# Window attention and two MLPs on one core: the last two weight pairs take turns over the token groups, and the first activations of the last product are loaded and made behind the last units

## The chip, the cores and the metric

The program runs on one core of a Trainium2 chip, in one launch. The metric is device microseconds (us) of that core, from the start of an execution to its end. The kernel before takes 907.42 us, the median of three runs (906.17 to 907.88).

## The reference, cut

```python
# q, k, v: 4 x 8 heads x 576 x 64; scale 1/8
mask = (rel >= 0) & (rel < 64)                  # rel = query position - key position
attn = softmax(where(mask, scale * q @ k.T, -1e9))
x = (attn @ v) -> 2304 tokens x 512
h = x @ w_in;  x = maximum(0.01 * h, h) @ w_out         # MLP 1: 512 -> 2048 -> 512
h = x @ w_in2; g = maximum(h, 0) + log1p(exp(-abs(h)))  # MLP 2: softplus
out = g @ w_out2                                        # 2048 -> 512
```

All inputs are float64 on the host. The kernel reads the weights as 64-bit words and makes two parts out of each number, a high one (type fp32r) and a low one, so that a product of two numbers takes three matmuls on TensorE: high by high, high by low, low by high (`three`, L469 to L471).

## The kernel before, in words

**Stages.** First the attention and MLP 1, mixed with each other; then the first product of MLP 2 (x by w_in2); then its second product (softplus of that, by w_out2). The change touches the end of the first product and the start of the second.

**The first product, by units.** The 2048 columns of h stand in 16 blocks of 128, two of which are a *pair* (p = 0 to 7). The 2304 tokens stand in three groups of 768 (c = 0 to 2). A *unit* is one pair on one group: `products(n, p, c)`, L526, 24 units in the order of a list written by hand (from L711 on): six units of pairs 0 and 1 mixed, then pair by pair with the three groups of each. A unit multiplies a 2 by 2 block matrix with seven half-size products instead of eight (L535 to L556); each product is 6 matmuls of 384 columns into a PSUM bank of its own, so a unit is 42 matmuls on TensorE, and takes it 7.33 us. The banks are eight, in turns (L531). What leaves the banks: one copy by ScalarE (`q1`, L547) and seven additions by VectorE (L545; `u2`, `u3`, `v` and four that write the unit's result h). The result goes to DRAM (`hd[p]`, L557, issued on SyncE's queue). The inputs of group c stand in seven wide tiles, `XB[c]` (`xb_c_n`), the seven weight combinations of a pair in `wp_..` rows (`pair_rows`, L208; made by `conv_pair`).

**The blocks of w_out2.** Behind and among the last units, the 16 row blocks of w_out2 (128 x 512 each) are converted, block j in four steps by a `ticker` (`last`): `load_w` (a DMA on SyncE's queue, L133, into one of three buffers `raw64`), `conv_a` (ScalarE, L159; reads the raw words, writes `cvp`), `conv_b` (VectorE: a shift L170 and an addition of the low word L176), `conv_c` (`split`: ScalarE casts the high part, L222, VectorE subtracts it from the number, L223). `conv_a` has two forms. As long as no softplus has been placed in the program (`softplus_on` is empty) it is an activation by a table, L159, that keeps the sign. Later it is a multiplication, L161, and `conv_b` then has one more VectorE instruction, L172, that puts the sign in. The places of the two parts come from `w2_rows`, L189: blocks 0 to 2 in two tiles of their own, blocks 3 to 5 in small buffers left over from the attention and the pairs (`pair_rows(8)`), the others in wide tiles `w2_n`, three rows in each. There are 21 wide places in all (`WIDE`), and a new wide tile takes the place of an older one, once the readers of that one are done.

**The second product, by steps.** The tokens stand in four chunks of 512 and one of 256; a step is one chunk and one block j, 80 steps (`second`, L584). A step of 512 tokens is 12 matmuls of 512 columns (L469 to L471, tile `f`). Its input is made by `load_h` (L568: 128 x 512 of `hd`, DRAM to `s0`, on SyncE's queue) and `activate` (L573): VectorE sets the sign bit (L576), ScalarE does the softplus of minus the absolute value (L577), VectorE adds max(h, 0) (L579), and then comes a `split` (L222 on ScalarE, L223 on VectorE). The tiles for it (`s0` to `s5`, six wide places) are taken in `second_places`, L559. Activations run SKEW = 2 steps ahead of `second`, loads three more.

**What sets the order.** Each engine runs its own queue, in order. A scheduler puts the instructions into the queues as the program issues them, by when it takes their inputs to be ready. `later` (L669) issues a piece of work no earlier than the end of the evacuation of the unit LAG2 = 3 behind. In the kernel before, `second_places`, all loads of `s0` and all activations are issued after the loop over the units.

In profile rows, a name with numbers left out stands for all tiles of the name: `cvp` a block in conversion, `w2xh` and `w2_n` its parts, `p_a`, `p_s` the banks of a unit, `q`, `u`, `h_xl` what comes out of them, `s` the tiles of the activations, `f` the banks of the second product.

Of the kernel before, what the change touches and what calls it, by code (L numbers as in the profile page):

```python
# [20 lines left out]
def tile_window_attention_two_mlps(  # L21
# [31 lines left out]
    NT, DM = out.shape  # L53
# [3 lines left out]
    NF = DFF // P  # L57
# [5 lines left out]
    SKEW = 2  # L63
# [6 lines left out]
    NX = NT // (2 * TH)  # L70
    TO = 512
# [116 lines left out]

    def w2_rows(j):  # L189


        if j < 3:
            if j == 0:
                w_rows["x"] = [x_tile(nm, f"w2{nm}", [P, 3, DM], F32R) for nm in ("xh", "xl")]
            return [w[:, j] for w in w_rows["x"]]
        if j < 6:
            if j == 3:
                w_rows["a"] = pair_rows(NF // 2)
            return [w.rearrange("p a b -> p (a b)") for w in w_rows["a"][2 * (j - 3) : 2 * (j - 3) + 2]]
        rows = []  # L200
        for n in (2 * (j - 6), 2 * (j - 6) + 1):
            if n % 3 == 0:
                w_rows["w", n // 3] = wide(f"w2_{n // 3}")
            rows.append(w_rows["w", n // 3][:, n % 3])
        return rows

    def pair_rows(p):

        row = lambda tag, bufs, n: sb.tile(
            [P, n, 2, DM // 2], F32R, tag=tag, bufs=bufs, name=f"wp_{p}_{tag}{len(got)}"  # L210
        )
        got = []
        tags = (("v", 3, 1), ("kT", 2, 1), ("qbd", 1, 2), ("part", 1, 3))
        if p % 2 == 0:
            tags = (("raw", 2, 1),) * 2 + (("v", 3, 1),) * 2 + (("sm", 2, 1),) * 2 + (("kT", 2, 1),)
        for tag, bufs, n in tags:
            t = row(tag, bufs, n)
            got += [t[:, i] for i in range(n)]
        return got
# [339 lines left out]
    def second_places():  # L559
        h, g, gh, gl, r0, r1 = (  # L560
            wide(f"s{n}", F32R if n in (2, 3) else F32) for n in range(6)
        )
        rows = lambda t: [t[:, n] for n in range(3)]
        stage["in"], stage["g"] = turns(rows(h)), turns(rows(g))
        stage["gs"] = turns(list(zip(rows(gh), rows(gl))))
        stage["res"] = turns(rows(r0) + rows(r1))

    def load_h(t0, n, j):  # L568
        h = next(stage["in"])[:, :n]
        nc.sync.dma_start(h, hd[j // 2][:, j % 2, t0 : t0 + n])  # L570
        return h
# [137 lines left out]


    order = [(0, 0), (0, 1), (1, 0), (0, 2), (1, 1), (1, 2)]  # L711
    order += [(p, c) for p in range(2, NF // 2) for c in range(NX)]
    last_of = {p: max(n for n, (q, _) in enumerate(order) if q == p) for p in range(NF // 2)}
    todo = {n: [] for n in range(len(order))}
    todo[0] += [(load_x, 2, 0)]
# [2 lines left out]
    for p in range(2, NF // 2):  # L718
# [1 line left out]
        todo[n - 1] += [(next, first[p])] * 4  # L720
        todo[n] += [(next, first[p], None)] * 2
        todo[n + 1] += [(conv_pair, p)]
    for n, k in ((-6, 4), (-5, 2), (-3, 4), (-2, 4), (-1, 4)):
        todo[len(order) + n] += [(next, last)] * k
    for n, (p, c) in enumerate(order):
        products(n, p, c)
        for f, *a in todo[n]:
            later(f, *a)

    chunks = [(t0, min(TO, NT - t0)) for t0 in range(0, NT, TO)]  # L730
    steps2 = [(k, t0, n, j) for k, (t0, n) in enumerate(chunks) for j in range(NF)]
    loaded, active = {}, {}
    second_places()
    for i in range(-3, len(steps2) + SKEW):
        if 0 <= i < len(steps2):
            active[i] = activate(steps2[i][2], loaded.pop(i))
        if i + 3 < len(steps2):
            k, t0, n, j = steps2[i + 3]
            loaded[i + 3] = load_h(t0, n, j)
        if i >= 0:  # L740
            for _ in range(2):
                later(next, last, None)
        if i >= SKEW:
            second(*steps2[i - SKEW], active.pop(i - SKEW))


# [28 lines left out]
```

## Time and profile before

| | |
|---|---|
| median of three runs | 907.42 us (906.17 to 907.88) |
| the profiled execution's own time | 906.67 us |
| its span, first to last instruction | 904.6 us |
| TensorE matmuls (PE) busy | 870.0 us, 96% |
| TensorE weight loads (PEld) busy | 818.4 us, 90% |
| VectorE (DVE) busy | 538.2 us, 59% |
| ScalarE (ACT) busy | 419.7 us, 46% |
| GpSimd (POOL) busy | 47.7 us, 5% |
| mean granted TensorE clock | 0.985 |

The profile is of one execution, and its span is 2.07 us shorter than that execution's time. The busy shares are means over stages that differ. The views read below are the page's clock line, the list of who an engine waits for, the timelines of single engines, and a table of busy times by stretches of the span.

### The profile page before, as it was taken

How to read it: one execution, taken by the hardware profiler on the slowest of the kernel's cores; microseconds unless marked ns; L12 is line 12 of the kernel's file. 1: busy time of each engine (PE TensorE's matmuls, PEld its weight loads, DVE VectorE, ACT ScalarE, POOL GpSimd, SP SyncE). 2: the span in 40 equal slices, each digit the busy share in tenths (PEclk: the TensorE clock that was granted, in tenths of full speed). 3: DMA queues.
4: the chain of work that ended last, by engine and by line, in shares of the span. 5: the costliest groups of instructions: out<-in, count | busy, mean ns of one | idle time of the engine just before them, and what ended most of it. 6: DMA issues, size and time to landing. Idle time of an engine off the chain costs nothing.

```text
span 904.6 us, 14252 instructions
## 1 busy us (share of the span) xinstructions
PE 870.0 (96%) x5232; PEld 818.4 (90%) x5232; DVE 538.2 (59%) x1055; ACT 419.7 (46%) x990; POOL 47.7 (5%) x66
## 2 busy tenths in 40 slices
PE   5699999999999999999999999999995999999998
PEld 4498999999999999999999999999995788888886
DVE  3898852534333333333257599777889767667664
ACT  4888752654444443543446433222235544544443
POOL 2211000211100101100000000000000000000000
PEclk8899999999999999999999999999998899999999
DMA  6667742243232311110132245444667434344432
GB/s 174 182 183 219 233 107 33 73 72 76 48 56 53 84 48 46 48 24 1 37 129 80 95 153 186 151 151 152 216 226 279 129 94 141 102 141 117 126 99 67
DMA packets 150277, 104.74 MB, mean 116 GB/s; under 512 B 104896, under 2 KB 129472, under 8 KB 150208
## 3 DMA queue, kind: packets, MB, share of 16 engines
q1 hardware_dynamic: 150208, 103.84, 39.9%
q8 instruction: 41, 0.67, 0.3%
q14 instruction: 28, 0.23, 0.1%
HBM read 75.50 MB, written 28.31 MB: 115 GB/s over the span
## 4 chain that ended last, share of the span: by engine, by line
PE 93%; DVE 2%; DMA 2%; ACT 2%; issue 1%; POOL 0%; POOLq 0%; DVEq 0%; ACTq 0%; SPq 0%
PE ph L469 7%; PE f L469 7%; PE f L471 7%; PE f L470 7%; PE o L469 7%; PE o L470 7%; PE o L471 7%; PE ph L470 7%; PE ph L471 7%; PE ps L382 4%; PE p_s L469 4%; PE p_s L471 4%; PE p_s L470 4%; PE p_a L469 3%; PE p_a L471 3%; PE p_a L470 3%
## 5 line engine op out<-in xcount | busy, mean ns | idle before, releaser
L485 DVE TENSOR_TENSOR gl<-g,gh 128x384 fp32r<-128x384 f32 x96 | 58.6, 611 | 159.1 <-ACT gh L484 158.6
L469 PE MATMUL ph<-xh,w 128*128 128x384 f32 x384 | 132.3, 345 | 0.0
L469 PE MATMUL o<-gh,w 128*128 128x384 f32 x384 | 131.7, 343 | 0.0
L470 PE MATMUL o<-gl,w 128*128 128x384 f32 x384 | 129.8, 338 | 0.0
L470 PE MATMUL ph<-xl,w 128*128 128x384 f32 x384 | 129.0, 336 | 0.0
L471 PE MATMUL ph<-xh,w 128*128 128x384 f32 x384 | 128.8, 335 | 0.0
L471 PE MATMUL o<-gh,w 128*128 128x384 f32 x360 | 121.7, 338 | 0.0
L481 ACT ACTIVATE g<-ph 128x384 f32<-128x384 f32 x96 | 46.9, 489 | 134.6 <-PE ph L471 134.5
L577 ACT ACTIVATE s<-s 128x512 f32<-128x512 f32 (+1 forms) x80 | 46.8, 588 | 75.2 <-DVE s L576 74.6
L579 DVE SCALAR_TENSOR_TENSOR s<-s,s 128x512 f32<-128x512 f32 (+1 forms) x80 | 50.7, 638 | 42.5 <-ACT s L577 42.3
L469 PEld LDWEIGHTS ph<-xh,w 128*128 128x128 f32 x384 | 72.1, 188 | 0.9
L470 PEld LDWEIGHTS ph<-xl,w 128*128 128x128 f32 x384 | 72.2, 188 | 0.2 <-DVE xl L426 0.2
L470 PEld LDWEIGHTS o<-gl,w 128*128 128x128 f32 x384 | 72.2, 188 | 0.0
L469 PEld LDWEIGHTS o<-gh,w 128*128 128x128 f32 x384 | 72.2, 188 | 0.0
L471 PEld LDWEIGHTS ph<-xh,w 128*128 128x128 f32 x384 | 72.1, 188 | 0.0
L392 ACT ACTIVATE sm<-sm,nm 128x128 f32<-128x128 f32 x144 | 56.1, 391 | 34.1 <-DVE nm L389 33.9
L469 PE MATMUL f<-w,s 128*128 128x512 f32 x180 | 70.0, 389 | 0.0
L470 PE MATMUL f<-w,s 128*128 128x512 f32 x180 | 70.0, 389 | 0.0
L471 PE MATMUL f<-w,s 128*128 128x512 f32 x180 | 70.0, 389 | 0.0
L471 PEld LDWEIGHTS o<-gh,w 128*128 128x128 f32 x360 | 67.6, 188 | 0.0
L223 DVE TENSOR_TENSOR s<-s,s 128x512 fp32r<-128x512 f32 (+1 forms) x80 | 50.9, 637 | 15.4 <-ACT s L222 15.1
L222 ACT CAST s<-s 128x512 fp32r<-128x512 f32 (+1 forms) x80 | 46.1, 578 | 22.7 <-PE f L470 22.4
(171 smaller groups left out, 1754.0 us busy)
## 6 DMA issues: line engine op xcount, KB each, us to landing
wraw<-in_moe_w_in_dram SPq DMA_DIRECT2D x32, 512.0 KB, 4.8
wraw<-in_moe_w_out_dram SPq DMA_DIRECT2D x32, 512.0 KB, 4.5
s<-hd SPq DMA_DIRECT2D x64, 256.0 KB, 2.7
hd<-h_xh SPq DMA_DIRECT2D x12, 768.0 KB, 4.5
hd<-h_xl SPq DMA_DIRECT2D x12, 768.0 KB, 4.3
x2d<-x SPq DMA_DIRECT2D x24, 192.0 KB, 1.9
x_stage<-x2d SPq DMA_DIRECT2D x24, 192.0 KB, 2.5
out_dram<-s SPq DMA_DIRECT2D x18, 256.0 KB, 2.3
```

Source lines behind the costliest of these rows:

```text
L222: i = nc.scalar.copy(hi, a)
L223: j = nc.vector.tensor_tensor(lo, a, hi.bitcast(F32), ALU.subtract)
L382: nc.tensor.matmul(ps[:, p, :], qbd[:, p, u, :], kT[t][:, p, w0 : w0 + P], start=True, stop=True,)
L392: a = nc.scalar.activation(sm[:, p, :], sm[:, p, :], AF.Exp, bias=nm[:, p : p + 1], accum_out=sums[:, p : p + 1],)
L469: nc.tensor.matmul(ps, wh, xh, start=start, stop=False)
L470: nc.tensor.matmul(ps, wh, xl, start=False, stop=False)
L471: nc.tensor.matmul(ps, wl, xh, start=False, stop=stop)
L481: nc.scalar.activation(g, ph, AF.Prelu, alpha=0.01)
L485: b = nc.vector.tensor_tensor(gl, g, gh.bitcast(F32), ALU.subtract)
L577: nc.scalar.activation(g, g, AF.Softplus)
L579: nc.vector.scalar_tensor_tensor(g, h, 0.0, g, ALU.max, ALU.add)
```

## The change

The list of units is written in another order for the last two pairs: instead of (6,0), (6,1), (6,2), (7,0), (7,1), (7,2), pair and group, it is now (6,0), (7,0), (6,1), (7,1), (6,2), (7,2). `second_places` and the first three loads of `s0` are issued behind unit 20 (N - 4), the first activation and the fourth load behind unit 22, the second activation and the fifth load behind unit 23; the loop over the steps then makes the others, as before two steps ahead. The conversion of w_out2's blocks is spread in another way over the last units (3, 3, 4, 4, 2 ticks behind units 18 to 22, instead of 4, 2, 0, 4, 4, 4 behind 18 to 23). Blocks 3 to 5 of w_out2 now stand in wide tiles as well. In the changed kernel, line numbers from `w2_rows` on are 5 lower (`split` is L217 and L218, the units' additions L540, `activate` L571 to L574).

```diff
     def w2_rows(j):
...
-        if j < 6:
-            if j == 3:
-                w_rows["a"] = pair_rows(NF // 2)
-            return [w.rearrange("p a b -> p (a b)") for w in w_rows["a"][2 * (j - 3) : 2 * (j - 3) + 2]]
         rows = []
-        for n in (2 * (j - 6), 2 * (j - 6) + 1):
+        for n in (2 * (j - 3), 2 * (j - 3) + 1):
...
     order = [(0, 0), (0, 1), (1, 0), (0, 2), (1, 1), (1, 2)]
-    order += [(p, c) for p in range(2, NF // 2) for c in range(NX)]
+    order += [(p, c) for p in range(2, NF // 2 - 2) for c in range(NX)]
+
+    order += [(p, c) for c in range(NX) for p in range(NF // 2 - 2, NF // 2)]
...
-    for n, k in ((-6, 4), (-5, 2), (-3, 4), (-2, 4), (-1, 4)):
-        todo[len(order) + n] += [(next, last)] * k
+
+    chunks = [(t0, min(TO, NT - t0)) for t0 in range(0, NT, TO)]
+    steps2 = [(k, t0, n, j) for k, (t0, n) in enumerate(chunks) for j in range(NF)]
+    loaded, active = {}, {}
+
+    def load_next(i):
+        if i < len(steps2):
+            k, t0, n, j = steps2[i]
+            loaded[i] = load_h(t0, n, j)
+
+    def activate_next(i):
+        if i < len(steps2):
+            active[i] = activate(steps2[i][2], loaded.pop(i))
+
+
+    N = len(order)
+    todo[N - 6] += [(next, last)] * 3
+    todo[N - 5] += [(next, last)] * 3
+    todo[N - 4] += [(second_places,)] + [(load_next, i) for i in range(3)] + [(next, last)] * 4
+    todo[N - 3] += [(next, last)] * 4
+    todo[N - 2] += [(activate_next, 0), (load_next, 3), (next, last), (next, last)]
+    todo[N - 1] += [(activate_next, 1), (load_next, 4)]
     for n, (p, c) in enumerate(order):
         products(n, p, c)
         for f, *a in todo[n]:
             later(f, *a)
 
-    chunks = [(t0, min(TO, NT - t0)) for t0 in range(0, NT, TO)]
-    steps2 = [(k, t0, n, j) for k, (t0, n) in enumerate(chunks) for j in range(NF)]
-    loaded, active = {}, {}
-    second_places()
-    for i in range(-3, len(steps2) + SKEW):
-        if 0 <= i < len(steps2):
-            active[i] = activate(steps2[i][2], loaded.pop(i))
-        if i + 3 < len(steps2):
-            k, t0, n, j = steps2[i + 3]
-            loaded[i + 3] = load_h(t0, n, j)
-        if i >= 0:
-            for _ in range(2):
-                later(next, last, None)
-        if i >= SKEW:
-            second(*steps2[i - SKEW], active.pop(i - SKEW))
+    for i in range(len(steps2)):
+        activate_next(i + SKEW)
+        load_next(i + SKEW + 3)
+        for _ in range(2):
+            later(next, last, None)
+        second(*steps2[i], active.pop(i))
```

ScalarE's queue around the end of the units, before. `cvp_1_15` is block 15 in conversion, `q1_23` the copy of the last unit's first bank, `s1` and `s2` the tiles of the activations:

```order
L547 COPY q1_23_7211<-p_23_a11_7215 128x384
L222 CAST w2_2_7205<-cvp_1_10_7200 128x512
L159 ACTIVATE cvp_1_12_7280<-wraw_1_12_1_7194 128x512
L222 CAST w2_3_7275<-cvp_1_11_7201 128x512
L159 ACTIVATE cvp_1_13_7281<-wraw_1_13_1_7203 128x512
L159 ACTIVATE cvp_1_14_7295<-wraw_1_14_1_7273 128x512
L222 CAST w2_4_7290<-cvp_1_12_7280 128x512
L222 CAST w2_4_7290<-cvp_1_13_7281 128x512
L222 CAST w2_5_7298<-cvp_1_14_7295 128x512
L159 ACTIVATE cvp_1_15_7296<-wraw_1_15_1_7283 128x512
L577 ACT_TABLE_LOAD
L577 ACTIVATE s1_7305<-s1_7305 128x512 x3
```

The same place after:

```order
L161 ACTIVATE cvp_1_12_7228<-wraw_1_12_1_7136 128x512
L572 ACT_TABLE_LOAD
L572 ACTIVATE s1_7014<-s1_7014 128x512
L542 COPY q1_23_7239<-p_23_a11_7243 128x384
L572 ACTIVATE s1_7014<-s1_7014 128x512
L217 CAST s2_7015<-s1_7014 128x512
L217 CAST w2_5_7223<-cvp_1_11_7143 128x512
L217 CAST w2_6_7313<-cvp_1_12_7228 128x512
L161 ACTIVATE cvp_1_13_7229<-wraw_1_13_1_7145 128x512
L161 ACTIVATE cvp_1_14_7319<-wraw_1_14_1_7221 128x512
L217 CAST s2_7015<-s1_7014 128x512
```

The table load and the first softplus have moved from behind the conversion of block 15 to the place between the conversion of block 12 and the copy of the last unit; blocks 12 to 15 are converted by L161 instead of L159.

VectorE's queue in unit 19, before. `p_19_..` are the unit's banks, `cvp_1_2`, `cvp_1_3` and `cvp_1_4` the blocks 2 to 4 of w_out2:

```order
L545 TENSOR_TENSOR u2_19_6872<-p_19_s2_6883,q1_19_6871 128x384
L545 TENSOR_TENSOR u3_19_6873<-p_19_s3_6891,u2_19_6872 128x384
L545 TENSOR_TENSOR v_19_6874<-p_19_s1_6899,u2_19_6872 128x384
L545 TENSOR_TENSOR h_xl_5444<-p_19_s1_6899,u3_19_6873 128x384
L545 TENSOR_TENSOR h_xl_5444<-p_19_a12_6908,q1_19_6871 128x384
L545 TENSOR_TENSOR h_xl_5444<-p_19_s4_6916,v_19_6874 128x384
L545 TENSOR_TENSOR h_xl_5444<-p_19_a22_6924,u3_19_6873 128x384
L223 TENSOR_TENSOR w2xl_6936<-cvp_1_2_6941,w2xh_6935 128x512
L170 TENSOR_SCALAR cvp_1_3_6942<-cvp_1_3_6942 128x512
L170 TENSOR_SCALAR cvp_1_4_7081<-cvp_1_4_7081 128x512
L176 SCALAR_TENSOR_TENSOR cvp_1_3_6942<-wraw_1_3_1_6866,cvp_1_3_6942 128x512
```

After:

```order
L170 TENSOR_SCALAR cvp_1_3_6942<-cvp_1_3_6942 128x512
L176 SCALAR_TENSOR_TENSOR cvp_1_2_6941<-wraw_1_2_1_6861,cvp_1_2_6941 128x512
L540 TENSOR_TENSOR u2_19_6867<-p_19_s2_6878,q1_19_6866 128x384
L176 SCALAR_TENSOR_TENSOR cvp_1_3_6942<-wraw_1_3_1_6928,cvp_1_3_6942 128x512
L540 TENSOR_TENSOR u3_19_6868<-p_19_s3_6886,u2_19_6867 128x384
L218 TENSOR_TENSOR w2xl_6936<-cvp_1_2_6941,w2xh_6935 128x512
L540 TENSOR_TENSOR v_19_6869<-p_19_s1_6894,u2_19_6867 128x384
L540 TENSOR_TENSOR h_xl_5444<-p_19_s1_6894,u3_19_6868 128x384
L540 TENSOR_TENSOR h_xl_5444<-p_19_a12_6903,q1_19_6866 128x384
L218 TENSOR_TENSOR w2_0_7033<-cvp_1_3_6942,w2_0_7033 128x512
L540 TENSOR_TENSOR h_xl_5444<-p_19_s4_6911,v_19_6869 128x384
L540 TENSOR_TENSOR h_xl_5444<-p_19_a22_6919,u3_19_6868 128x384
```

The conversion of block 3 has moved from behind the additions of unit 19 to places ahead of them and between them.

VectorE's queue behind the last addition of unit 23 (`a22_23`), before:

```order
L545 TENSOR_TENSOR h_xl_5444<-p_23_a22_7264,u3_23_7213 128x384
L170 TENSOR_SCALAR cvp_1_12_7280<-cvp_1_12_7280 128x512
L170 TENSOR_SCALAR cvp_1_13_7281<-cvp_1_13_7281 128x512
L176 SCALAR_TENSOR_TENSOR cvp_1_12_7280<-wraw_1_12_1_7194,cvp_1_12_7280 128x512
L176 SCALAR_TENSOR_TENSOR cvp_1_13_7281<-wraw_1_13_1_7203,cvp_1_13_7281 128x512
L170 TENSOR_SCALAR cvp_1_14_7295<-cvp_1_14_7295 128x512
L223 TENSOR_TENSOR w2_4_7290<-cvp_1_12_7280,w2_4_7290 128x512
L223 TENSOR_TENSOR w2_5_7298<-cvp_1_13_7281,w2_4_7290 128x512
L176 SCALAR_TENSOR_TENSOR cvp_1_14_7295<-wraw_1_14_1_7273,cvp_1_14_7295 128x512
L223 TENSOR_TENSOR w2_5_7298<-cvp_1_14_7295,w2_5_7298 128x512
L170 TENSOR_SCALAR cvp_1_15_7296<-cvp_1_15_7296 128x512
L576 TENSOR_SCALAR s1_7305<-s0_7304 128x512
```

After:

```order
L540 TENSOR_TENSOR h_xl_5444<-p_23_a22_7292,u3_23_7241 128x384
L574 SCALAR_TENSOR_TENSOR s1_7014<-s0_7013,s1_7014 128x512
L571 TENSOR_SCALAR s1_7014<-s0_7013 128x512
L218 TENSOR_TENSOR w2_6_7313<-cvp_1_12_7228,w2_6_7313 128x512
L218 TENSOR_TENSOR s3_7016<-s1_7014,s2_7015 128x512
L574 SCALAR_TENSOR_TENSOR s1_7014<-s0_7013,s1_7014 128x512
L170 TENSOR_SCALAR cvp_1_13_7229<-cvp_1_13_7229 128x512
L170 TENSOR_SCALAR cvp_1_14_7319<-cvp_1_14_7319 128x512
L172 SCALAR_TENSOR_TENSOR cvp_1_13_7229<-wraw_1_13_1_7145,cvp_1_13_7229 128x512
L218 TENSOR_TENSOR s3_7016<-s1_7014,s2_7015 128x512
L176 SCALAR_TENSOR_TENSOR cvp_1_13_7229<-wraw_1_13_1_7145,cvp_1_13_7229 128x512
L172 SCALAR_TENSOR_TENSOR cvp_1_14_7319<-wraw_1_14_1_7221,cvp_1_14_7319 128x512
```

The activations of the first two steps now stand directly behind the last addition, and the conversion of blocks 13 and 14 with the new L172 behind and between them; blocks 12 to 15 followed first before.

## Rows read from the trace of the kernel before

**Rows 1.** Page, part 2: granted TensorE clock in 40 slices of the span, in tenths.
```profile
PEclk8899999999999999999999999999998899999999
```

**Rows 2.** Who TensorE waits for, whole span: total us, times, longest us.
```profile
PE pt L408 <- POOL sm L399: 10.5, 7, 3.4
...
PE f L469 <- ACT s L222: 10.5, 1, 10.5
```

**Rows 3.** Timeline, TensorE, 688 to 718: start us, length us, instruction, [idle before, releaser].
```profile
691.08 0.34 PE L471 MATMUL p_a<-xb,wp_qbd 128*128 128x384 f32 x1
701.88 0.80 PE L469 MATMUL f<-w2xh,s 128*128 128x512 f32 x1 [10.46 <-ACT s L222]
...
707.24 0.40 PE L469 MATMUL f<-w2xh,s 128*128 128x512 f32 x1
...
715.45 0.39 PE L469 MATMUL f<-wp_v,s 128*128 128x512 f32 x1
```

**Rows 4.** Stretches: sums of busy us of PE, PEld, DVE, ACT, POOL; PEclk, DMA, GB/s.
```profile
21.10:28.00 6.90, 4.65 (x49) 4.04 (x48) 4.58 (x10) 6.31 (x23) 1.44 (x2) 1.00 0.37 78
34.70:41.50 6.80, 4.64 (x43) 3.21 (x41) 5.70 (x12) 4.20 (x10) 1.04 (x1) 0.50 0.36 116
...
655.45:662.50 7.05, 7.05 (x42) 7.05 (x41) 4.89 (x10) 2.13 (x4) 0.00 (x0) 1.00 0.62 226
662.50:691.30 28.80, 28.80 (x166) 28.60 (x164) 27.70 (x56) 12.17 (x21) 0.00 (x0) 1.00 0.78 266
691.30:701.88 10.58, 0.12 (x2) 0.01 (x1) 8.94 (x18) 7.16 (x12) 0.00 (x0) 0.60 0.61 220
701.88:707.24 5.36, 5.36 (x12) 3.96 (x13) 4.90 (x10) 3.41 (x7) 0.00 (x0) 0.51 0.48 147
707.24:715.45 8.21, 8.21 (x37) 6.76 (x36) 5.23 (x10) 3.46 (x6) 0.00 (x0) 1.00 0.53 148
```

**Rows 5.** Timeline, ScalarE, of the conversions and the first softplus.
```profile
656.49 0.67 ACT L159 ACTIVATE cvp<-wraw 128x512 f32<-128x512 f32 x1 [1.64 <-DMA wraw<-in_moe_w_out_dram]
...
697.67 0.66 ACT L159 ACTIVATE cvp<-wraw 128x512 f32<-128x512 f32 x1 [0.77 <-DMA wraw<-in_moe_w_out_dram]
698.35 1.28 ACT L577 ACT_TABLE_LOAD   x1
699.64 1.67 ACT L577 ACTIVATE s<-s 128x512 f32<-128x512 f32 x3
```

**Rows 6.** Timelines: VectorE's last split for pair 7, TensorE's first matmul of unit 19.
```profile
648.47 0.69 DVE L223 TENSOR_TENSOR wp_part<-tt,wp_qbd 128x512 fp32r<-128x512 f32 x1
...
654.55 0.33 PE L469 MATMUL p_a<-xb,wp_raw 128*128 128x384 f32 x1
```

**Rows 7.** Timeline, VectorE, in units 19 to 23 and behind them.
```profile
655.45 0.42 DVE L170 TENSOR_SCALAR cvp<-cvp 128x512 int32<-128x512 int32 x1
...
677.82 0.42 DVE L170 TENSOR_SCALAR cvp<-cvp 128x512 int32<-128x512 int32 x1
678.17 0.69 DVE L223 TENSOR_TENSOR w<-cvp,w 128x512 fp32r<-128x512 f32 x1
678.78 0.75 DVE L176 SCALAR_TENSOR_TENSOR cvp<-wraw,cvp 128x512 uint16<-128x512 uint32 x1
679.42 0.54 DVE L545 TENSOR_TENSOR u<-p_s,q 128x384 f32<-128x384 f32 x1
...
688.90 0.55 DVE L545 TENSOR_TENSOR h_xl<-p_s,u 128x384 f32<-128x384 f32 x1
689.37 0.55 DVE L545 TENSOR_TENSOR h_xl<-p_a,q 128x384 f32<-128x384 f32 x1
...
691.93 0.75 DVE L170 TENSOR_SCALAR cvp<-cvp 128x512 int32<-128x512 int32 x2
...
700.33 1.89 DVE L579 SCALAR_TENSOR_TENSOR s<-s,s 128x512 f32<-128x512 f32 x3
```

**Rows 8.** The loads of raw weight blocks issued at L133 (32 in the program).
```profile
DMA to landing us min/median/max: 3.4/4.5/6.3
```

## The prediction

> **What bounds the kernel now.** I read the page's clock line first: the granted clock is full in nearly all of the 40 slices; it dips early, in the attention, and once near slice 31 [rows 1]. Then the list of who TensorE waits for: behind the attention it has one wait left, 10.5 us for ScalarE's cast at L222 [rows 2]. Everything else behind the attention is TensorE's own work, so the time moves only if that one place moves. TensorE's timeline gives its edges: the last matmul of the last unit (unit 23) starts at 691.08, and its successor would start some 0.17 later, at 691.25; the first matmul of the second product starts at 701.88 [rows 3]. The first step (12 matmuls, one block j) then lasts 5.36 us, until 707.24; the three steps behind it last 8.21, until 715.45, that is 2.74 each [rows 3]. The table by stretches says why: the clock granted was 0.60 in the hole and 0.51 in the first step, half rate (1.2 GHz), and 1.00 (2.4 GHz) afterwards [rows 4]. So the place costs 10.63 us of waiting and 2.62 of slow matmuls. **13.25 us** is all there is to gain.
>
> What ends the wait is seen on ScalarE: the conversion of the last weight block (L159) waits for its load until 697.67, the table load follows at 698.35, and then the first three softplus at 699.64 [rows 5]. And VectorE, which has to finish the units, convert the blocks and make the activations, waits for only 1.1 us of the 28.8 between 662.50 and 691.30 [rows 4]. It is full already, and the change gives it more to do there. That decides the size.
>
> **The turns of the last two pairs.** Same matmuls, same pitch. The weights of pair 7 are now needed in unit 19 instead of 21. Their last split starts on VectorE at 648.47 and takes 0.69; unit 19 starts on TensorE at 654.55 [rows 6]. They are 5.4 us early, and order and durations are unchanged up to there, so this costs nothing. The new order frees the first token group's seven tiles two units sooner, which is what lets the loads of the activations go out in unit 19. Cost on the path: 0. The rows of w2_out for blocks 3 to 5 move from odd corners into those tiles: same splits, cost 0.
>
> **The activations made early.** Here the term is counted on VectorE, instruction by instruction, because its queue runs in order. I take pitches (start to next start) where it runs without a wait [rows 7]: an add of a unit 0.47 (688.90 to 689.37), L170 0.35, a split L223 0.61, L176 0.64 (677.82 to 679.42), L579 0.60 (three in 1.89 us). L576 is like L170, one tensor in and out: 0.35.
>
> First the method on the kernel before: from 655.45, behind the last add of unit 18, to 691.93, behind the last add of unit 23, are 36.48 us [rows 7]. In them stand 35 adds (16.45), 10 L170 (3.50), 10 L176 (6.40), 10 splits (6.10), together 32.45, and so 4.0 us of waits. The stretches say 2.16 (655.45 to 662.50) and 1.10 (662.50 to 691.30) [rows 4], 3.3. The count is good to some 0.7 us.
>
> Now the queue of the changed kernel from the same point, up to L579 of step 4 (the fifth step): 35 adds 16.45; 14 L170 and 6 L576, 20 x 0.35 = 7.00; 14 L176 and **4 new ones** of another kind, 18 x 0.64 = 11.52; 17 splits, 13 of weights and 4 of activations, 10.37; 5 L579, 3.00. Sum 48.34. The four new ones: conv_b's branch for blocks that are converted after the first softplus has been placed (12 to 15), which never ran before. It is bounded by L170's 0.35 and by the longest VectorE instruction in these rows, 0.75; it has two tensors in like L176, so I take 0.64.
>
> Waits: unit 19 had 2.16 of them. Blocks 2 and 3 are now converted ahead of and between its adds (2.2 us of instructions from behind it), but the first of these has to wait for block 3's load, whose L159 starts only at 656.49 [rows 5]; until it is done, at about 657.2, some 1.3 us go by. That leaves 1.3, and of the 1.10 later perhaps 0.8: 2.1 in all. From L579's end to the first matmul it was 701.88 - 700.33 - 0.60 = 0.95 us (cast and hand-over) [rows 3, 7].
>
> Step 4 therefore starts at 655.45 + 48.34 + 2.1 + 0.95 = **706.84**. In the kernel before it starts at 715.45 [rows 3]. From there on both run at TensorE's pitch (it never waits again, [rows 2]), so the gain is **8.6 us**. The steps between, by the same count: step 0 ready at 688.7, before TensorE is free at 691.25; step 1 ready at 695.1 (TensorE free 694.0), step 2 at 697.3 (free 697.8), step 3 at 702.7 (free 700.6), step 4 at 706.8 (free 705.4). TensorE waits three times, 1.1, 2.1 and 1.4 us, and each time it has worked in between. Step 5 is ready 1.2 us behind step 4 on VectorE, well inside TensorE's 2.74, so the queue has caught up.
>
> What is late next is thus VectorE, with blocks 13 to 15 converted between the activations of steps 1 to 4. The adds of a late unit cost TensorE nothing: a bank is used again eight products, over a unit, later. The h stores and the three early loads on SP share the transfer engines at 0.62 to 0.78 [rows 4]; a raw block takes 4.5 us to land at the median [rows 8], and blocks 13 to 15 are issued long before VectorE comes to them. Cost 0 while that holds.
>
> **ScalarE's queue.** The table load and the first softplus now stand in front of unit 23's q1 copy, and behind the conversion of block 12. VectorE's adds of unit 23 wait for that copy. By the count, block 9's L176 is done at 679.5, so load 12 goes out then and lands 4.8 us later at 684.3; conversion 0.67, table load 1.28, softplus 0.63 end at 686.9, and VectorE gets there at 687.2. Cost 0, with 0.3 us to spare.
>
> The table load itself: ScalarE's conversion ends at 697.67 + 0.66 = 698.33, the load starts at 698.35, and the softplus follows 1.29 later [rows 5]. There is no pause in front of it. The Trainium skill, "ScalarE: Activation LUTs", section on what ACT_TABLE_LOAD costs, adds about 1.38 us of draining to the 1.28. By that, an estimate, unit 23's adds would start 1.1 us later and the gain would be 7.5; the row decides, and the sum keeps 1.28.
>
> **The bounds.** Waits from 1.0 (unit 19 filled wholly) to 4.0 (as before), the four new instructions from 0.35 to 0.75: step 4 between 704.6 and 709.2, gain 10.9 to 6.3.
>
> The profiled execution took 906.67 us (span 904.6 and 2.07 around it), 0.75 below the median 907.42 of the three runs. 906.67 - 8.6 = 898.1; I say **898.2**, and for the bounds alone 895.8 to 900.4.
>
> **The rivals.**
> 1. *Nothing is late, the whole 13.25 us go:* 893.4. It needs VectorE to have spare room; the 1.1 us of waits in 28.8 speak against it. 5 in 100.
> 2. *The clock.* The three short waits make TensorE drop to half rate. For it: the clock fell behind the long wait [rows 4], and in the attention it was granted at 0.50 in 34.70 to 41.50. Against it: in 21.10 to 28.00, where TensorE waited several times but briefly, it was 1.00 [rows 4]; the 3.4 us longest attention wait [rows 2] is above all three that I expect. Price: steps 1 to 3 at 5.36 from 695.1 on put step 4 at 711.2, a gain of 4.3: 902.4. 10 in 100. The Trainium skill, "TensorE: Matmul & The Clock Gate", section on HAM oscillation, warns that bursts with waits between them can each start at the low rate; that is this rival.
> 3. *Slower.* The in-order queue of ScalarE: load 12, queued on SP behind unit 21's store, lands late, and the conversion holds up table load, softplus and the q1 copy, and VectorE's adds and all activations behind them. Past the 0.3 us to spare each us costs one; the gain is gone when it takes 8.9 us longer, and the kernel is 1.8 us slower at 10.7 longer (15 us to land): 908.5 and above. The longest of 32 landings was 6.3 [rows 8]. 4 in 100.
> 4. *It doesn't do what it says:* only step 0 is made early in full, and if the two engines' waits for each other add up to some 8 us in steps 1 to 4, nothing is left: within 0.2% of before. 3 in 100.
>
> **How the numbers follow.** The forecast with its bounds has 72 in 100, 6 lie between it and the last two rivals. The range 895.5 to 902.5 takes in the bounds and the clock rival and leaves out about 15 in 100. About 0.2% (1.8 us) is what a measurement of this kernel can tell from no change. Faster by more than that 0.93, within it 0.03, slower 0.04.
>
> **What would show it.** TensorE goes from unit 23 to the first step without a wait, then waits 3 to 6 us in all before step 4, for ScalarE's cast at L217; step 4 starts near 707; the clock line has no dip near slice 31; VectorE is full from 662 to about 707; ScalarE has the table load near 685, before unit 23's copy. It is wrong if TensorE waits before step 0, if the half rate appears, if TensorE waits in unit 19 for pair 7, or if the waits sum to under 2 us or over 8.

## The result

| kernel | median, us | runs | ratio to before, 95% interval |
|---|---|---|---|
| before | 906.79 (905.99 to 907.88) | 4 | |
| changed | 898.84 (897.46 to 899.65) | 4 | 0.991 (0.9892 to 0.9928) |

The change takes 7.95 us off; by the interval, 6.5 to 9.8. The forecast was 898.2, between 895.5 and 902.5.

The profiled execution of the changed kernel took 899.1 us, its span is 897.1. First its list of who TensorE waits for (total us, times, longest), whole span, and the clock line of its page:

```profile
PE f L464 <- ACT s L217: 3.6, 3, 1.7
PEclk9799999999999999999999999999999999999999
```

The one wait of 10.5 us [rows 2] has become three of 3.6 us together, and the dip near slice 31 [rows 1] is gone. TensorE's timeline has the edges (start us, length us, instruction, [idle before, releaser]):

```profile
692.30 0.33 PE L466 MATMUL p_a<-xb,wp_qbd 128*128 128x384 f32 x1
692.47 0.39 PE L464 MATMUL f<-w2xh,s 128*128 128x512 f32 x1
...
696.17 0.50 PE L464 MATMUL f<-w2xh,s 128*128 128x512 f32 x1 [0.78 <-ACT s L217]
...
703.64 0.50 PE L464 MATMUL f<-w,s 128*128 128x512 f32 x1 [1.67 <-ACT s L217]
...
707.78 0.50 PE L464 MATMUL f<-w,s 128*128 128x512 f32 x1 [1.11 <-ACT s L217]
```

The last matmul of unit 23 starts at 692.30 (691.08 before, [rows 3]); step 0 follows it at the pitch of a matmul, and steps 1, 3 and 4 wait. The last unit ends 1.22 us later than in the profile of before. That is not put down to the change: the start lies between 690.24 and 692.56 in the profiles of the table below, whose kernels all have the same attention and first MLP. So the place itself is measured from there to the end of the span, which the table does for every kernel (one profile of each, where the times are medians of four runs or more):

| kernel | last matmul of unit 23 starts | span | from there to the end | against before |
|---|---|---|---|---|
| before | 691.08 | 904.6 | 213.52 | |
| changed | 692.30 | 897.1 | 204.80 | -8.72 |
| e1 turns only | 691.58 | 905.5 | 213.92 | +0.40 |
| e2 early only | 692.56 | 898.8 | 206.24 | -7.28 |
| e3 no sign | 691.26 | 897.0 | 205.74 | -7.78 |
| e4 two signs | 690.24 | 898.4 | 208.16 | -5.36 |
| e5 GpSimd, from block 6 | 692.03 | 898.4 | 206.37 | -7.15 |
| e6 loads only, first form | 691.16 | 895.3 | 204.14 | -9.38 |
| e6b loads only | 691.87 | 896.9 | 205.03 | -8.49 |
| e7 GpSimd, loads only | 691.34 | 896.9 | 205.56 | -7.96 |
| e8 ticks only | 690.58 | 897.6 | 207.02 | -6.50 |
| e9 half pace | 691.77 | 896.2 | 204.43 | -9.09 |
| e10 half pace, fewer before | 691.85 | 892.1 | 200.25 | -13.27 |
| e11 before, with the pace alone | 691.66 | 892.7 | 201.04 | -12.48 |

VectorE's timeline of the changed kernel, from the last addition of unit 18 to the activation of step 4:

```profile
656.67 0.43 DVE L170 TENSOR_SCALAR cvp<-cvp 128x512 int32<-128x512 int32 x1
658.21 0.43 DVE L170 TENSOR_SCALAR cvp<-cvp 128x512 int32<-128x512 int32 x1 [1.11 <-ACT cvp L159]
...
672.12 0.43 DVE L170 TENSOR_SCALAR cvp<-cvp 128x512 int32<-128x512 int32 x1 [0.28 <-ACT cvp L159]
...
680.44 0.43 DVE L170 TENSOR_SCALAR cvp<-cvp 128x512 int32<-128x512 int32 x1 [0.73 <-ACT cvp L159]
...
687.89 0.68 DVE L172 SCALAR_TENSOR_TENSOR cvp<-wraw,cvp 128x512 int32<-128x512 int32 x1
688.49 0.68 DVE L574 SCALAR_TENSOR_TENSOR s<-s,s 128x512 f32<-128x512 f32 x1
...
694.80 0.67 DVE L574 SCALAR_TENSOR_TENSOR s<-s,s 128x512 f32<-128x512 f32 x1
...
706.27 0.67 DVE L574 SCALAR_TENSOR_TENSOR s<-s,s 128x512 f32<-128x512 f32 x1
```

It waits three times, 2.1 us in all, each time for a conversion on ScalarE, and has no other pause of note from 656.67 to the end of the last row at 706.94. The L574 at 688.49 is step 0's and stands ahead of unit 23's additions; directly behind the last of these stand those of steps 1 (694.80) and 2, not those of the first two steps, as the section on the change has it. TensorE's list names ScalarE's cast (L217), but ahead of step 1's cast ScalarE had itself waited for the L574 at 694.80:

```profile
695.50 0.62 ACT L217 CAST s<-s 128x512 fp32r<-128x512 f32 x1 [2.25 <-DVE s L574]
```

Two of the stretches (columns as in [rows 4]) show VectorE full in the units and behind them, and the full clock beside a wait of TensorE:

```profile
662.50:691.30 28.80, 28.80 (x167) 28.80 (x166) 27.67 (x56) 14.88 (x25) 0.00 (x0) 1.00 0.83 285
700.00:703.00 3.00, 1.98 (x9) 1.31 (x7) 3.00 (x7) 1.90 (x4) 0.00 (x0) 1.00 0.00 1
```

### The profile page after: what moved, and what is told of

It reads as the page before. It is cut to its first block, busy times and chain, and to the rows that moved or that the text cites. A ratio compares the mean times of both kernels' runs of the same rounds, so it can differ in the third digit from the quotient of the medians.

```text
span 897.1 us, 14253 instructions
## 1 busy us (share of the span) xinstructions
PE 870.1 (97%) x5232; PEld 818.0 (91%) x5232; DVE 538.8 (60%) x1059; ACT 419.5 (47%) x990; POOL 47.5 (5%) x66
## 4 chain that ended last, share of the span: by engine, by line
PE 91%; DVE 4%; DMA 2%; ACT 1%; issue 1%; POOL 0%; POOLq 0%; DVEq 0%; ACTq 0%; SPq 0%
PE ph L464 7%; PE o L464 7%; PE o L465 7%; PE o L466 7%; PE ph L465 7%; PE ph L466 7%; PE f L464 7%; PE f L465 7%; PE f L466 7%; PE ps L377 4%; PE p_s L464 3%; PE p_s L466 3%; PE p_s L465 3%; PE p_a L464 3%; PE p_a L466 2%; PE p_a L465 2%
## 5 line engine op out<-in xcount | busy, mean ns | idle before, releaser
L464 PE MATMUL f<-w,s 128*128 128x512 f32 x234 | 91.3, 390 | 2.8 <-ACT s L217 2.8
L465 PE MATMUL f<-w,s 128*128 128x512 f32 x234 | 91.1, 389 | 0.0
L466 PE MATMUL f<-w,s 128*128 128x512 f32 x234 | 90.7, 389 | 0.0
L572 ACT ACTIVATE s<-s 128x512 f32<-128x512 f32 (+1 forms) x80 | 47.0, 589 | 69.3 <-DVE s L571 68.7
L574 DVE SCALAR_TENSOR_TENSOR s<-s,s 128x512 f32<-128x512 f32 (+1 forms) x80 | 50.8, 636 | 38.5 <-ACT s L572 38.1
L218 DVE TENSOR_TENSOR s<-s,s 128x512 fp32r<-128x512 f32 (+1 forms) x80 | 50.8, 636 | 13.9 <-ACT s L217 13.7
L217 ACT CAST s<-s 128x512 fp32r<-128x512 f32 (+1 forms) x80 | 46.2, 577 | 24.9 <-PE f L465 19.5
```

Of the source, the lines that this page charges most:

```text
L217: i = nc.scalar.copy(hi, a)
L218: j = nc.vector.tensor_tensor(lo, a, hi.bitcast(F32), ALU.subtract)
L464: nc.tensor.matmul(ps, wh, xh, start=start, stop=False)
L465: nc.tensor.matmul(ps, wh, xl, start=False, stop=False)
L466: nc.tensor.matmul(ps, wl, xh, start=False, stop=stop)
L572: nc.scalar.activation(g, g, AF.Softplus)
```

## The experiments

Each kernel ran against the kernel before on the same chip; times are medians. The theory: the sum of VectorE's queue through the activation of step 4 sets the gain. The rivals: the turns, the early loads, the early activations, or the landing of raw blocks do.

**The parts of the change, one by one.** e1 is the kernel before with the new order of units and wide tiles for blocks 3 to 5:

```diff
-    order += [(p, c) for p in range(2, NF // 2) for c in range(NX)]
+    order += [(p, c) for p in range(2, NF // 2 - 2) for c in range(NX)]
+    order += [(p, c) for c in range(NX) for p in range(NF // 2 - 2, NF // 2)]
...
-        if j < 6:
...
-        for n in (2 * (j - 6), 2 * (j - 6) + 1):
+        for n in (2 * (j - 3), 2 * (j - 3) + 1):
```

> The kernel before with one part of the change alone: the last two pairs take turns, and blocks 3 to 5 of w_out2 stand in wide tiles (which the turns need, since pair 6's small buffers are in use for longer). Places, loads and activations of the second product are issued after all units, as before. Theory (VectorE's queue through the fifth step of the second product sets the gain): nothing of that queue is shortened, so TensorE keeps one wait of about 10.5 us before the first step and the half clock behind it, and the time stays within 1.5 us of 906.8. Rival (the turns themselves help, since tiles come free two units sooner and the loads of raw blocks or of the activations start sooner): the wait is shorter than 8.5 us and the time is at most 904.5.

It takes 906.71 us, ratio 0.9999 (0.9988 to 1.001), and TensorE's wait is the old one:

```profile
PE f L465 <- ACT s L218: 10.9, 1, 10.9
```

The turns alone bring nothing and cost nothing. e2 is the other half: the changed kernel with the lines of that diff put back.

> The changed kernel with the pairs in their old order (and blocks 3 to 5 in their old places): places, loads and activations early, no turns. The loads of the activations then have to wait for unit 21's first product instead of unit 19's. Theory (VectorE's queue): the same instructions stand on VectorE, the loads still land some 8 us before the first activation is due, and only the order of the queue suffers a little from loads of raw blocks queued behind them: the waits of TensorE before the fifth step sum to 4 to 7 us, time 899 to 902. Rival (the turns are what makes the early loads possible): waits near those of before, 905 or more.

900.24 us, ratio 0.992 (0.9904 to 0.9937), within the theory's range; the intervals can't tell it from the changed kernel's 0.991. Two rows of TensorE's timeline and a stretch:

```profile
698.69 0.65 PE L468 MATMUL f<-w2xh,s 128*128 128x512 f32 x1 [3.04 <-ACT s L221]
...
709.50 0.50 PE L468 MATMUL f<-wp_v,s 128*128 128x512 f32 x1 [0.73 <-ACT s L221]
700.00:703.00 3.00, 3.00 (x10) 2.38 (x9) 3.00 (x7) 1.03 (x2) 0.00 (x0) 0.62 0.36 136
```

Its waits sum to 3.8 us, a little less than the 4 to 7 expected, but the first is one of 3.04, and behind it the granted clock is 0.62, the half rate (1.2 GHz) for most of a step. In the place it is 1.44 us behind the changed kernel, in one profile of each; whether the turns bring that, by the tiles' earlier release, is not shown. e6 and e6b keep the early loads and put the first activations behind all units (the diff is that of e6b):

```diff
-    todo[N - 2] += [(activate_next, 0), (load_next, 3), (next, last), (next, last)]
-    todo[N - 1] += [(activate_next, 1), (load_next, 4)]
+    todo[N - 2] += [(next, last), (next, last)]
...
+    for i in range(SKEW):
+        activate_next(i)
+        load_next(i + 3)
     for i in range(len(steps2)):
```

> The changed kernel, but the first two activations are issued behind all units: places and loads early, activations late. Blocks 12 and 13 then go by the table again, so two of the four L172 vanish (1.2 us). Theory (VectorE's queue through the fifth step): the sum of that queue does not depend on where in it the first activations stand, so what is lost before the first step (a wait of 2 to 3 us there) comes back at the later ones, waits 3 to 4 us in all, time 897.5 to 899.3. Rival (the early activations are the gain, since they give TensorE its first steps at once and keep its clock up): a wait of 5 us or more before the first step, with half clock behind it, 902 or more.

> As e6_loads_only, with the fourth and fifth load of an activation issued behind the first and second activation, whose places they take (in e6 they were issued ahead of them, so that the first two steps multiplied other blocks of h than they should). Theory (VectorE's queue): as e6: one wait of about 2.1 us before the first step, half clock in that step, 897.4 to 898.6. Rival (e6 was fast only because its first activations did not wait for what they should): 900 or more.

e6 takes 897.88 us, ratio 0.9897 (0.9882 to 0.9911), e6b 897.95, ratio 0.9888 (0.9872 to 0.9905). Timeline and stretches of e6b:

```profile
695.13 0.50 PE L464 MATMUL f<-w2xh,s 128*128 128x512 f32 x1 [2.92 <-ACT s L217]
697.00:700.00 3.00, 3.00 (x9) 2.31 (x9) 3.00 (x7) 1.72 (x3) 0.00 (x0) 0.60 0.93 313
```

One wait of 2.92 us ahead of the first step, half rate behind it (0.60), and nothing later. By the intervals the time can't be told from that with the first activations made early, so making them early is not what gains. e6's first two steps multiply other blocks of h than they should, so e6b is the one to go by. Of the theory, the time is right, but the later waits that were expected of e6 did not come in either: one wait and the half rate behind it make up the sum. e8 is the kernel before with the spread of the ticks alone:

```diff
-    for n, k in ((-6, 4), (-5, 2), (-3, 4), (-2, 4), (-1, 4)):
+    for n, k in ((-6, 3), (-5, 3), (-4, 4), (-3, 4), (-2, 2)):
```

> The kernel before with one part of the change alone: the ticks of w_out2's conversion as in the changed kernel (3, 3, 4, 4, 2 behind units 18 to 22, then two for each step), so that blocks 14 and 15 are converted behind the first activations instead of ahead of them. No turns; places, loads and activations are issued behind all units. Theory (VectorE's queue): some 3 us of conversion leave the queue ahead of the first activation, and so does the wait for the last block's load, which in the kernel before ends at 697.67: the one wait shrinks from 10.5 to 4 to 6 us, with half clock behind it: 900.5 to 902.5. Rival (the early loads and the turns carry the gain): a wait of 8 us or more, 904.5 or above.

901.74 us, ratio 0.9931 (0.9914 to 0.9949). Its wait and the stretch behind it:

```profile
695.37 0.50 PE L469 MATMUL f<-w2xh,s 128*128 128x512 f32 x1 [4.45 <-ACT s L222]
697.00:700.00 3.00, 3.00 (x9) 2.33 (x9) 3.00 (x7) 1.21 (x2) 0.00 (x0) 0.57 0.35 129
```

One line, without turns, early places, loads or activations, brings 6.50 of the 8.72 us of the place; by the medians it is 5.5 of 8.0 (the profile is of e8's fastest execution). What it moves is the last part of the conversion (blocks 14 and 15, and what was left of 12 and 13), from ahead of the first activations to behind or between them. It also brings earlier blocks forward: 14 ticks stand behind units 18 to 21, where there were 10.

**More and less in VectorE's queue.** e3 leaves L172 out, and with it the sign of the weights in blocks 12 to 15; e4 has it twice:

```diff
             nc.vector.scalar_tensor_tensor(
                 ai, words(raw, I32)[1], -(2**31), ai, ALU.bitwise_and, ALU.bitwise_or
             )
+            nc.vector.scalar_tensor_tensor(
+                ai, words(raw, I32)[1], -(2**31), ai, ALU.bitwise_and, ALU.bitwise_or
+            )
```

> The changed kernel with L172 issued twice for blocks 12 to 15 (the second time changes nothing in the result): four more VectorE instructions of 0.60 to 0.67 us ahead of the fifth step's activation. Theory (VectorE's queue): 2.4 us more in that queue, so TensorE's waits before the fifth step grow from 3.6 to 5.5 to 6.1 us; if one of them passes 2 us, the half clock comes with it, as it did behind the waits of 2.0 to 3.0 us in the first four experiments and not behind those of 0.8 to 1.7 us in the changed kernel: 900.8 to 903.5. Rival (the raw blocks' landing sets the steps): 898.8, waits as they were.

901.17 us, ratio 0.993 (0.9915 to 0.9944): 2.33 us above the changed kernel for 2.4 us of VectorE's instructions (the intervals overlap), and 3.36 in the place. One of the three waits is now 2.31 us and has half rate behind it:

```profile
PE f L467 <- ACT s L220: 5.2, 3, 2.3
...
695.65 0.61 PE L467 MATMUL f<-w2xh,s 128*128 128x512 f32 x1 [2.31 <-ACT s L220]
697.00:700.00 3.00, 3.00 (x10) 2.39 (x9) 3.00 (x7) 0.62 (x1) 0.00 (x0) 0.62 0.80 256
...
707.44 0.75 DVE L577 SCALAR_TENSOR_TENSOR s<-s,s 128x512 f32<-128x512 f32 x1
```

The half rate is not what the 3.36 us are. The last row is the L574 of step 4 (L577 here): it starts 707.44 - 690.24 = 17.20 us behind the last unit, in the changed kernel 706.27 - 692.30 = 13.97, so 3.2 later: 2.4 of new instructions, and VectorE's own waits for conversions are 3.0 us, not 2.1. TensorE waits for VectorE again ahead of steps 3 and 4, and what the half rate took is lost in these waits.

> The changed kernel without L172, the four new VectorE instructions (so the sign of w_out2's blocks 12 to 15 is left out). All four stand ahead of the fifth step's last activation, each 0.60 to 0.67 us. Theory (VectorE's queue): 2.4 us leave the queue ahead of the fifth step, TensorE waited for 3.6 us in its three waits, so the waits shrink to 1.2 to 2.0 us and the time to 896.4 to 897.3. Rival (landing of the raw blocks, or the table load on ScalarE, sets the steps): nothing changes, 898.8.

898.16 us, ratio 0.9897 (0.9882 to 0.9912), a miss: the theory wanted 897.3 at most, and in the place e3 is 0.94 us worse than the changed kernel. VectorE's and TensorE's timelines and the stretches show where it went:

```profile
701.88 0.69 DVE L572 SCALAR_TENSOR_TENSOR s<-s,s 128x512 f32<-128x512 f32 x1
703.11 0.68 DVE L572 SCALAR_TENSOR_TENSOR s<-s,s 128x512 f32<-128x512 f32 x1
...
703.33 0.50 PE L462 MATMUL f<-w,s 128*128 128x512 f32 x1 [2.02 <-ACT s L215]
703.00:706.00 3.00, 2.67 (x8) 2.16 (x9) 3.00 (x7) 1.53 (x4) 0.00 (x0) 0.72 0.55 160
706.00:709.00 3.00, 3.00 (x11) 2.32 (x11) 1.78 (x4) 1.86 (x4) 0.00 (x0) 0.71 0.06 20
```

L572 of e3 is L574 of the changed kernel. Step 4's starts 703.11 - 691.26 = 11.85 us behind the last unit, against 13.97: 2.1 us sooner, near the theory's 2.4. But the order of the queue is another: step 3's starts 10.62 behind it, against 9.92 (702.22), so TensorE, which waits for 0.9 us within step 1, waits for 2.02 ahead of step 3, and the clock falls to 0.72 and 0.71 in the stretches behind it. Step 3 is late, and at half rate, so step 4 can't use what VectorE's queue got back.

**The work moved to another engine.** e5 is the changed kernel, e7 is e6b, with the low parts of blocks 6 to 15 subtracted by GpSimd:

```diff
-        split(hi, lo, a)
+        split(hi, lo, a, nc.gpsimd if m == 1 and i == 1 and j >= 6 else None)
```

> The changed kernel, but the low parts of w_out2's blocks 6 to 15 (L218) are subtracted by GpSimd instead of VectorE: ten instructions of 0.60 us less in VectorE's queue, ten on GpSimd, where the nearest row (128 x 512, L399 of the kernel before) takes 1.08 us. Theory (VectorE's queue): 6.0 us leave the queue, more than the 3.6 us of waits, so TensorE waits for less than 1 us in all; 894.3 to 895.6. Rival (GpSimd and VectorE hold each other up at the memory): VectorE's instructions get longer beside GpSimd's, by 0.3 us or more each, and the time stays at 897.5 or above. The Trainium skill, 'trace-analysis', says that the two share a read port and that moving work between them might not help; this is that rival.

> Loads early and activations late, as e6b, and the low parts of blocks 6 to 15 on GpSimd, as e5. Theory (VectorE's queue): the queue ahead of the first activation is shorter by the splits of blocks 6 to 11 (3.6 us), more than the 2.1 us of e6b's wait, so the first step follows the last unit with less than 0.5 us of waiting, and no later step waits: 894.0 to 895.2. Rival (GpSimd holds VectorE up): the wait before the first step stays at 2 us or more with half clock behind it, 897.5 or above.

899.72 us, ratio 0.9917 (0.9896 to 0.9938), and 898.65, ratio 0.9902 (0.9887 to 0.9917): by the times the rival, both times. e5's waits sum to 2.7 us, one of 1.49 with half rate behind it (granted clock 0.66 between 697 and 700). e7's way there is not the rival's, though: its wait before the first step is 0.55 us, not 2, four short ones follow, and the granted clock is 1.00 in all its stretches from 655 to 712:

```profile
PE f L466 <- DVE s L218: 2.4, 4, 0.9
PE f L464 <- ACT s L217: 0.5, 1, 0.5
```

What holds of the rival is that VectorE's instructions get longer. The groups of instructions between 662 and 709 (busy us, mean ns), first of the changed kernel, then of e5:

```profile
L218 DVE TENSOR_TENSOR w<-cvp,w 128x512 fp32r<-128x512 f32 x13 | 8.8, 684 | 0.1
L176 DVE SCALAR_TENSOR_TENSOR cvp<-wraw,cvp 128x512 uint16<-128x512 uint32 x12 | 8.8, 750 | 0.0
L170 DVE TENSOR_SCALAR cvp<-cvp 128x512 int32<-128x512 int32 x12 | 4.9, 422 | 1.0 <-ACT cvp L159 1.0
L574 DVE SCALAR_TENSOR_TENSOR s<-s,s 128x512 f32<-128x512 f32 x6 | 4.0, 673 | 0.0
L571 DVE TENSOR_SCALAR s<-s 128x512 int32<-128x512 int32 x7 | 2.9, 411 | 0.0
...
L540 DVE TENSOR_TENSOR v<-p_s,u 128x384 f32<-128x384 f32 x4 | 2.2, 554 | 0.0
```

```profile
L176 DVE SCALAR_TENSOR_TENSOR cvp<-wraw,cvp 128x512 uint16<-128x512 uint32 x12 | 11.1, 943 | 0.1
L574 DVE SCALAR_TENSOR_TENSOR s<-s,s 128x512 f32<-128x512 f32 x6 | 6.3, 1046 | 0.0
L170 DVE TENSOR_SCALAR cvp<-cvp 128x512 int32<-128x512 int32 x12 | 6.0, 505 | 1.0 <-ACT cvp L159 1.0
L571 DVE TENSOR_SCALAR s<-s 128x512 int32<-128x512 int32 x7 | 3.7, 543 | 0.1
...
L540 DVE TENSOR_TENSOR v<-p_s,u 128x384 f32<-128x384 f32 x4 | 2.2, 550 | 0.0
L218 DVE TENSOR_TENSOR w<-cvp,w 128x512 fp32r<-128x512 f32 x3 | 2.1, 702 | 0.0
...
672.56 1.29 POOL L218 TENSOR_TENSOR w<-cvp,w 128x512 fp32r<-128x512 f32 x1 [238.54 <-ACT w L217]
672.62 1.86 DVE L176 SCALAR_TENSOR_TENSOR cvp<-wraw,cvp 128x512 uint16<-128x512 uint32 x1
```

Ten splits leave VectorE, 8.8 - 2.1 = 6.7 us. Four groups that read and write SBUF alone grow by 2.3, 2.3, 1.1 and 0.8, together 6.5 us; by the mean that is 0.08 to 0.37 us for each instruction, less than the rival's 0.3 for all but L574. The last two rows, of the timelines, show one case: L176 takes 1.86 us instead of 0.75 beside a GpSimd instruction of 1.29. The additions that read a PSUM bank (L540) keep their 0.55, also beside GpSimd. The work was given back in the same queue. The Trainium skill, "SBUF — State Buffer", section "SBUF: two separate sides", says that the two engines share a pair of ports that one instruction (of VectorE's, one with two inputs in SBUF, or in a mode with two ports) holds to its end while the other is fully blocked; the trace agrees, 1.86 being 0.75 and 1.11 more, beside 1.23 us of GpSimd's instruction.

**Less work ahead, not elsewhere.** Block j is not needed before step j. e9 is the changed kernel with a tick behind every second step, e10 also leaves out the two behind unit 22, and e11 is the kernel before with this alone:

```diff
-        for _ in range(2):
+        if i % 2 == 0:
             later(next, last, None)
```

e11 has also

```diff
-    for n, k in ((-6, 4), (-5, 2), (-3, 4), (-2, 4), (-1, 4)):
+    for n, k in ((-6, 3), (-5, 3), (-4, 4), (-3, 4)):
```

> The changed kernel with one tick of the conversion behind every second step instead of two behind every step; block j is needed only at step j, 2.74 us for each step later. Theory (VectorE's queue): of the conversions of blocks 13 to 15 (2.2 us each with L172) about two leave the queue ahead of the fifth step's activation, 4 us or more against 3.6 us of waits; what stays is the wait of about 0.8 us at the second step: 894.8 to 896.3. Rival (the conversions are needed where they are, since a step then waits for its block, or the queue is held by something else): 898 or more.

896.72 us, ratio 0.9881 (0.9863 to 0.9899), a little above what was expected. TensorE's one wait with the first matmuls of steps 1 and 2, and what VectorE waited for:

```profile
697.11 0.50 PE L464 MATMUL f<-w2xh,s 128*128 128x512 f32 x1 [2.25 <-ACT s L217]
...
701.56 0.39 PE L464 MATMUL f<-w2xh,s 128*128 128x512 f32 x1
...
DVE cvp L170 <- ACT cvp L159: 2.3, 2, 1.8
```

Steps 3 and 4 no longer wait. Step 1 does, for 2.25 us instead of 0.8: in this profile (of the slowest of e9's executions, 898.18 us) a raw block landed later, and VectorE stood still for 1.8 us ahead of it. Behind the wait the granted clock is 0.65 between 697 and 700, and step 1 lasts 701.56 - 697.11 = 4.45 us instead of 2.74 [rows 3]; these 1.7 us are what the half rate costs here.

> As e9, and the two ticks behind unit 22 are left out as well, so that two more ticks (with a block's conversion, 2.2 us) leave the queue ahead of the second step's activation. Theory (VectorE's queue): TensorE goes from the last unit through all steps without a wait of 0.3 us or more, the whole 13.25 us of the place are gone: 893.8 to 895.3. Rival (another engine or the landing of a late block then sets a step): a wait of 1 us or more at steps 5 to 15, 896 or more.

893.55 us, ratio 0.9848 (0.9833 to 0.9862), the fastest of all and a little below what was expected. TensorE's list from 60 us to the end has nothing of the second product left, and no stretch behind the units falls below the full clock; two of them:

```profile
694.20:697.00 2.80, 2.80 (x14) 2.33 (x13) 2.80 (x7) 1.89 (x4) 0.00 (x0) 1.00 0.99 315
709.00:725.00 16.00, 16.00 (x72) 13.23 (x72) 15.24 (x29) 8.58 (x16) 0.00 (x0) 1.00 0.38 120
```

The place gives back 13.27 us; the prediction counted 13.25 in it. VectorE is busy for 15.24 of the 16 us behind 709, so the conversions now fill the steps.

> The kernel before with the pace of the conversion alone: 3, 3, 4, 4 ticks behind units 18 to 21, then one behind every second step. No turns, no early places, loads or activations. Theory (VectorE's queue): the first activations come right behind the last additions, so the wait before the first step is below 1.5 us and later ones sum to 1.5 us at most: 895.0 to 897.5. Rival (the turns and the early loads are needed to have the activations in time): the first step waits for the loads of h, 3 us or more with half clock behind it, 899 or more.

894.82 us, ratio 0.986 (0.9843 to 0.9878), a little below what was expected, and the second product's share of the waits is

```profile
PE f L469 <- ACT s L222: 0.3, 1, 0.3
```

So the kernel before, with nothing but another pace of the conversion, is faster than the changed kernel by some 4 us. e10 and e11 can't be told apart by their intervals; in the place they are 0.79 us apart. The slower pace also takes conversions off ScalarE and loads off the queue, so e9 to e11 alone don't tell these from VectorE. That it is VectorE rests on e4, which adds to VectorE alone, and on the stretch of the changed kernel from 700 to 703, shown above, where TensorE waits: VectorE is busy for all 3.00 us, ScalarE for 1.90, and the DMA share is 0.00.

## Why the prediction was right, point by point

- **What bounds it.** Right: 13.25 us were in the place, and e10 gets 13.27 out.
- **The count on VectorE.** Right. From the last addition of unit 18 to the end of step 4's L574, 48.34 us of instructions and 2.1 of waits were counted, 50.4; the trace has 706.94 - 656.67 = 50.3, with 2.1 of waits, 1.11 of them in unit 19 (1.3 expected). The gain in the place is 8.72, 8.6 was forecast. The waits come at steps 1, 3 and 4, 0.78, 1.67 and 1.11 us; 1.1, 2.1 and 1.4 were worked out. The list leaves out some 0.3 us of each: against e10, which does not wait, the changed kernel loses 204.80 - 200.25 = 4.55 us in the place, against 4.6 worked out. e4 moved step 4 with the length of the queue. But step 4 is not the one to count to in every kernel: in e6b, e8 and e9 the activation of step 0 or 1 comes late, the half rate follows, and step 4's is then ready ahead of TensorE.
- **L172.** It lasts 0.68 us and its successor starts 0.60 behind it; 0.64 was taken between 0.35 and 0.75. Left out in e3, it makes step 4's activation 2.1 us sooner, but the time no better, since another step's wait then brings the half rate.
- **ScalarE's queue.** Right to 0.1 us. ScalarE's timeline of the changed kernel:

```profile
685.50 0.69 ACT L161 ACTIVATE cvp<-wraw 128x512 f32<-128x512 f32 x1 [2.23 <-DMA wraw<-in_moe_w_out_dram]
686.20 1.28 ACT L572 ACT_TABLE_LOAD   x1
687.50 0.63 ACT L572 ACTIVATE s<-s 128x512 f32<-128x512 f32 x1
```

  With the 1.22 us that the last unit is later, the first softplus was to end at 688.1 and VectorE to come to it at 688.4; it ends at 688.13 and L574 starts at 688.49. That it fits this well is partly luck: the 4.8 us to landing stand in no row ([rows 8] has 4.5 at the median), and load 12 was issued at 681.60, 0.9 later than the count has it, and was converted 3.9 later; the two errors cancel. There is 0.01 us between L161 and the table load, no pause, as in [rows 5].
- **The turns.** Cost 0, right (e1). But the text holds them to be what lets the loads go out in time, and the gain to come from activations made early. Here the reading was too narrow: without turns (e2) or without early activations (e6b) most of the gain is there, and with the ticks alone (e8) two thirds to three quarters. The count was right because it counts what stands ahead of step 4's activation, wherever the first ones stand; in the kernel before nearly the whole conversion of sixteen blocks stood ahead of the first one.
- **The clock rival.** It did not come in the changed kernel, whose stretches are all at 1.00, but it was near: the waits of 2.0 to 4.5 us in e2, e3, e4, e6b, e8 and e9 have half rate behind them. Its price was put too high, three steps at half rate (4.3 us): in e9 it is 1.7, and in e4 it is lost in later waits. The Trainium skill, "TensorE: Matmul & The Clock Gate", section on HAM oscillation, describes bursts that start at the low rate behind a wait; the runs agree, with 0.57 to 0.72 granted in the stretches behind these waits.
- **The other rivals.** Nothing was slower or the same. "Nothing is late" did not come true for this change, as VectorE had no room; e10 makes the room.

## What to carry to other kernels

When an engine's in-order queue ends a wait, count what stands in it up to the first instruction that the waiting engine has no slack for, and ask of each item when it is needed: here blocks 13 to 15, needed nine steps of 2.74 us and more behind step 4, were converted ahead of it, and a slower pace of that conversion was worth more than an order of units, early loads and early activations together. Moving such work to GpSimd gave the time back (e5, e7). Whether a few short waits are cheaper than one long one is not settled here: against e10, in the place, three of 3.6 us together cost 4.55 us (changed), one of 2.92 with half rate behind it 4.78 (e6b), and five of 2.9 together at full clock 5.31 (e7).

## What was not expected of the hardware

In e5, four groups of VectorE's instructions with SBUF operands alone got longer beside GpSimd's by nearly what the ten moved splits had taken (6.5 against 6.7 us), while the additions with a PSUM operand did not. GpSimd's own took 1.29 to 1.86 us each, and 9.13 for the last three together; the nearest row, L399 of the kernel before, an instruction on other tiles, takes 1.08. And the half rate came behind waits of 2.0 to 2.3 us (e3, e4, e9), not only behind ones of 10; in e5 it came behind one of 1.49 us with shorter breaks ahead of it, and in the changed kernel not behind 1.67, nor behind e7's five of up to 0.92. What exactly decides between these stays open.
